# SyncE's transfers kept in source order up to step 16, and one weight load asked for a step later, in a one-core adaLN + S4D + token-mixer kernel

## The chip, the cores and the metric

The kernel runs on one core of a Trainium2 chip, as one launch. The metric is the device time of that core in microseconds (us). Before the change three runs gave 663.74, 665.47 and 670.17 us; the median, 665.47 us, is the time to compare with. Below, PE is the matmul engine, DVE VectorE, ACT ScalarE, POOL GpSimd and SP SyncE, which computes nothing here and issues nearly all transfers between DRAM and on-chip memory.

## The reference

One sequence of L = 2048 tokens with D = 448 channels goes through two blocks, each with a layer norm that is scaled and shifted by vectors made from a condition `c`:

```python
mod = (silu(c) @ w_mod).reshape(1, 6, 1, 448)          # six modulation vectors of 448
sa, ca, ga, sb, cb, gb = (mod[:, k] for k in range(6))
h = layernorm(x) * (1 + ca) + sa
x = x + ga * s4d(h)                                     # long convolution, kernel of N = 256 states
h = layernorm(x) * (1 + cb) + sb
x = x + gb * mixer(h)                                   # gelu(W1 . h + b1), W2: 2048 -> 1792 -> 2048 tokens

def s4d(u):                                             # per channel d
    A, C = -exp(log_A_real) + 1j * A_imag, (C_real + 1j * C_imag) * exp(log_dt)
    K = 2 * real(sum_n C[d, n] * exp(A[d, n] * dt[d] * pos))       # pos = 0 .. 2047
    return causal_convolution(u, K) + u * D_skip
```

## The kernel before, in words

**The steps.** The convolution kernel K is made for 16 channels at a time, in 28 groups `g` of two half groups each, so 56 steps `s`. A step needs two products that PE forms from small tables: exponents (tile `lex`, 4 buffers, group `g` in buffer `g % 4`) and phases (tile `lph`, 3 buffers, group `g` in `g % 3`). ACT turns them into magnitudes and sines, POOL multiplies the tile `G` (L734, L735), DVE the tile `E` (L736 to L740), and PE contracts `E` with `G` into `kg` (L761). Steps come in batches of eight: ahead of each batch stands a window (`window(s)` for s = 8, 16, 24, 32) in which the exponentials of all eight steps are taken at once, because sines and exponentials need different tables on ACT.

**What goes on beside the steps.** From the window of step 8 to that of step 16, PE also transforms the input: `u_rows` multiplies a row of `xt` into PSUM, DVE scales the result into a tile `yt` (L592), and each two of these make one store to DRAM, `yu_d<-yt` (L594, 448 KB). There are 32 such rows, hence 16 stores; in the text below they are **store 1 to store 16**. The tiles `yt` have three buffers (stores 3 to 5 borrow room elsewhere and are called `yE`), so from store 9 on, DVE may write the tile of store k only when store k-3 has landed. From step 16 on, these 16 stores are read back (`u_load`) for the next transform (`u_cols`).

**Loads that fall into this stretch.** `load(g, False)` brings the phases of a group two groups ahead, in two transfers: `load_up` (L650, 32 partitions, 32 KB) and `load_lo` (L654, 64 partitions, 64 KB). `load(g, True)` does the same for exponents, and at steps 4, 12, 20 and so on it is called for four groups in a row, eight transfers. `wm_load(k, ...)` (L338) brings the weights of modulation vector k, 784 KB; those of k = 4, 5 and 3 go into rows 0 to 3, 4 to 7 and 8 to 11 of `xt`, once `u_rows` has used these, and are read by PE in the window of step 16 (L534). `par_load(3)` at step 12 brings the last parameters in eight transfers of 32 KB (L291).

**What sets the order.** On PE, ACT, DVE and POOL the instructions stand in the order of the source for the whole program. SP has that order only inside a context named `first`; outside of it, a scheduler places SP's instructions when the program is built, by when it thinks each can go. The context is entered early in the program and closed by `first.close()` in the loop over steps. The table `late` says at which step a weight load is called:

```python
if s % 2 == 0 and 0 < s and s // 2 + 2 < NG:
    load(s // 2 + 2, False)
if s == 8:
    first.close()
if s in late:
    late[s]()
if s % BATCH == 0:
    (late_window if s > 32 else window)(s)
```

SP works its list in order: an instruction that waits holds all behind it. Besides what its data need, nearly every transfer of SP waits for an earlier one: SP has eight completion semaphores that it uses in turn, and a transfer waits until the one eight places ahead of it in SP's list has landed.

Of the kernel before, what the change touches and what calls it, by code (L numbers as in the profile page):

```python
# [21 lines left out]
L, D, N, F = 2048, 448, 256, 1792  # L22
# [210 lines left out]
def tile_adaln_s4d_mixer(ctx, tc, i, out):  # L233
# [19 lines left out]
    with ExitStack() as es:  # L253
# [44 lines left out]
        PP = 112  # L298
# [6 lines left out]
        xt = xp.tile([P, 16, D], F32, name="xt")  # L305
# [30 lines left out]
        def wm_load(k, tile):  # L336
            wms[k] = tile
            nc.sync.dma_start(wms[k], i["w_mod"][:, k * D : (k + 1) * D].rearrange("(q p) d -> p q d", p=PP))  # L338
# [11 lines left out]
        def wm_slot(k):  # L350
# [16 lines left out]
            ],  # L367
            12: lambda: wm_load(4, xt[0:PP, 0:4, 0:D]),
            13: lambda: wm_load(5, xt[0:PP, 4:8, 0:D]),
            14: lambda: wm_load(3, xt[0:PP, 8:12, 0:D]),  # L370
        }


# [8 lines left out]
        def flush(todo):  # L382
            while todo:
                todo.pop(0)()
# [160 lines left out]
        def u_stats(r):  # L545
            st = xp.tile([P, 6], F32, tag="st", name="st", bufs=2)
            V.bn_stats(st, xt[:, r])
            V.bn_aggr(mv[:, r], st)
# [107 lines left out]
        def load(g, exps):  # L656
            load_up(g, exps)
            load_lo(g, exps)
# [12 lines left out]
        def warm(n):  # L671

            g = made_k[0] // 2
            free = (kgs[g - 1] if g - 1 in kgs else kg_tile(g))[:, 4:8]
            for _ in range(n):
                T.matmul(free, ones[:, 0:P], ones[:, 0:256], start=made_k[0] % 2 == 0, stop=made_k[0] % 2 == 0, skip_group_check=True)
# [7 lines left out]
        def st_exponents(s):  # L684
            g, h = divmod(s, 2)
            phs[s] = [pph.tile([P, 512], F32, tag=nm, name=nm) for nm in ("xe", "xg")]
            halves(phs[s], lex[g % 4][:, h * P : (h + 1) * P], tab[:, 2], True, True)
# [7 lines left out]
        def st_phase(s):  # L695

            g, h = divmod(s, 2)
            lhs = lph[g % 3][:, h * P : (h + 1) * P]
            pm = [pph.tile([P, 512], F32, tag=nm, name=nm) for nm in ("xe", "xg")]
            halves(pm, lhs, tab[:, 1], True, False)  # L700
            halves(pm, mg[:, 0], ones, False, False)
            halves(pm, mg[:, 1], ones, False, False)
            halves(pm, lhs, tab[:, 0], False, True)
            phs[s] = pm
# [43 lines left out]
        def mellow():  # L748
            ready.extend(fresh)
            fresh.clear()  # L750

        def st_kgen(s, to=act):
            g, h = divmod(s, 2)
            kg = kg_tile(g)
            made_k[0] += 1
            E, Gt = eg.pop(s)
            for m in range(4):
                for c in range(2):
                    for q in range(4):
                        d = 8 * (q // 2) + 2 * m + q % 2  # L760
                        T.matmul(  # L761
                            kg[32 * q : 32 * q + 32, m],
                            Gt[:, c, d],
                            E[:, c, d],
                            start=h == 0 and c == 0 and m == 0,
                            stop=h == 1 and c == 1,
                            skip_group_check=True,
                        )
            if h == 1:
                p, o = divmod(g, 2)  # L770
                if o == 0:
                    kss[p] = wp.tile([P, 2, 4, NJ], F32, tag="ks", name="ks")

                def copy():
                    (V.tensor_copy if to is dve else S.copy)(kss[p][:, o], kgs.pop(g)[:, 0:4])
                    if o:
                        dve.append(skip)

                def skip():
                    k0 = kss[p][:, :, :, 0:1]  # L780
                    G.tensor_tensor(k0, k0, dsk[:, g - 1 : g + 1, :, None], ALU.add)
                    fresh.append(p)

                to.append(copy)
# [62 lines left out]
        def pc_load(n):  # L847
            if n < NP:
                pc_u(n)
                pc_w(n)  # L850
            else:
                pc_u(2 * n - NP)
            pc_ahead(n - 4)
# [184 lines left out]
        def more(n):  # L1038

            for _ in range(n):  # L1040
                if next(rest, None) in ("logs", "end"):
                    return
# [120 lines left out]
        for s in range(NHALF):  # L1163
            if s == 32:
                early.close()
                fp = es.enter_context(tc.tile_pool(name="fp", bufs=2))
                m2p.append(right("m2l", BATCH - 3))
                yks[1] = fp.tile([P, 32, DC], F32, name="yk1", bufs=1)
                for n in range(3):
                    pc_load(n)  # L1170
            if s % 2 == 0 and 0 < s and s // 2 + 2 < NG:
                load(s // 2 + 2, False)
            if s == 8:
                first.close()
            if s in late:
                late[s]()
            if s % BATCH == 0:
                (late_window if s > 32 else window)(s)
                if s == 0:
                    gp_ = right("gp", 3)  # L1180
            if s % BATCH == 4:
                for g in range(s // 2 + 2, min(s // 2 + 6, NG)):
                    load(g, True)

            if s == 5:
                late_steps.append(True)

            def between():
                flush(dve)
                if 2 <= s < BATCH:  # L1190
                    for r in range(2 * s, 2 * s + 2):
                        u_stats(r)
                if s < len(pace):
                    more(pace[s])

            mellow()
            if True:
                if s < 32 and s % BATCH > 1:
                    st_kgen(s - 2)
                if s % BATCH == 1 or s < 24 and s % BATCH == 0:  # L1200
                    warm(10)
                if (s + 1) % BATCH:
                    st_phase(s + 1)
                elif s + 1 < NHALF:
                    st_exponents(s + 1)
                if s == 7:
                    warm(10)

                due.extend(soon)
                soon.clear()  # L1210
                if s > 32 and s % BATCH:
                    st_kgen(s - 1, soon)
                if s in (40, 48):
                    piece(True)
                    flush(dve)
                st_step(s, between)
                if s in (40, 48):
                    piece(False, True)
            if s == NHALF - 1:
                break  # L1220
            flush(act)

            if s in (1, 2):
                x_load(4 + 4 * s, 4, G)
            if s in (23, 31):
                idle(10)
            held = s > 32 and s % BATCH == BATCH - 2
            free = s > 7 and not st_s1(hold if held and s + 2 < NHALF else dve if s % BATCH == BATCH - 1 else act)
            if s + 2 < 32 and (s + 2) % BATCH > 1 and s + 2 > 5:
                st_mag2(s + 2)  # L1230

            if 3 < s < 8:
                modulation(s // 2 - 1, s % 2)
            if s == 7:
                par_load(2)

            if 8 <= s < 16 and free:
                some(u_rows, rows, 2 if s % 2 else 3)
            if s == 12:
                par_load(3)  # L1240
            if s == 16:
                spec.close()
                up = early.enter_context(tc.tile_pool(name="up", bufs=2))
                for n in range(4):
                    u_load(n)
                sp3 = early.enter_context(tc.tile_pool(name="sp3", bufs=1))
                s2_load(2, 8, sp3)
            if 17 <= s < 32 and free:
                some(u_cols, cols, 1)
            if s == 31:  # L1250
                flush(dve)
                flush(act)
            if s > 32 and not held and s not in (40, 48):
                piece(s % 2 == 1, back=s % BATCH != BATCH - 1)
            if s == 34:

                for t in (ft, b1, b2):
                    V.memset(t, 0.0)
                nc.sync.dma_start(ft, i["FT"])
                nc.sync.dma_start(b1, i["B_b1"].rearrange("(t p) -> p t", p=P))  # L1260
                nc.sync.dma_start(b2, i["B_b2"].rearrange("(t p) -> p t", p=P))
# [117 lines left out]
    with ExitStack() as es:  # L1379
# [169 lines left out]
        for t in range(16):  # L1549
            ss = slice(t * P, (t + 1) * P)  # L1550
            xt = ru.tile([P, D], F32, tag="x2", name="x2")
# [42 lines left out]
```

## Time and profile before

| what | value |
|---|---|
| median of the runs | 665.47 us (663.74, 665.47, 670.17) |
| the profiled execution's own time | 666.04 us |
| its span, first to last instruction | 664.3 us |
| mean granted TensorE clock | 0.987 |
| moved by DMA | 125.14 MB, mean 188 GB/s |

The span is what the profile's positions count in: "at 104.05" means 104.05 us after the first instruction. The 1.7 us between span and time lie outside of all instructions. A row of the timeline is: start, us (first start to last end of the rows merged in it), engine, line, operation, out<-in, how many, and in brackets the idle time of the engine before it and what ended that. For SP, whose rows are issues only, the start says when SP issued the transfer and not when the data arrived; the arrival is seen from who waited for it.

### The profile page before, as it was taken

The page shows a single profiled execution, that of the slowest core. Times are in us where ns is not written, and L with a number is a line of the kernel's source. Part 1 is how long each engine was busy: PE and PEld are TensorE (multiplying, and loading weights), DVE is VectorE, ACT ScalarE, POOL GpSimd, SP SyncE. Part 2 cuts the span into 40 slices and gives each one's busy share as a digit, 9 for nine tenths or more (in the row PEclk, how much of TensorE's full clock was granted, in tenths as well). Part 3 has the DMA queues.
Part 4 walks back from the last instruction along what each step waited for, and adds up shares of the span by engine and source line. Part 5 has one row for each costly group of instructions (what it writes and reads, how often), then busy time and mean ns, then how long its engine had stood idle before and what let it go on. Part 6 is the DMA issues. An engine that isn't in the chain of part 4 may idle for free.

```text
span 664.3 us, 19155 instructions
## 1 busy us (share of the span) xinstructions
PE 612.2 (92%) x7639; PEld 442.8 (67%) x7639; DVE 444.1 (67%) x852; ACT 440.9 (66%) x828; POOL 269.5 (41%) x350
## 2 busy tenths in 40 slices
PE   1868998999999999999898999999999999999997
PEld 0544455445455555656554667788999999999997
DVE  8999889798893877868665677787522553333331
ACT  6978898999889999999587578886222532222220
POOL 7885597498599788797562000000000000000000
PEclk9999999999999999999999989999999999999999
DMA  6695747598876457676787999946665165555530
GB/s 159 195 222 171 271 136 245 213 269 238 230 263 190 66 160 204 186 210 193 236 279 218 257 241 232 218 117 195 181 179 149 59 197 165 162 160 163 166 113 28
DMA packets 98833, 125.14 MB, mean 188 GB/s; under 512 B 13780, under 2 KB 80120, under 8 KB 98744
## 3 DMA queue, kind: packets, MB, share of 16 engines
q1 hardware_dynamic: 97928, 121.30, 64.6%
q0 software_dynamic: 816, 2.62, 1.6%
q8 instruction: 60, 0.98, 0.7%
q14 instruction: 29, 0.24, 0.1%
HBM read 88.53 MB, written 34.87 MB: 186 GB/s over the span
## 4 chain that ended last, share of the span: by engine, by line
PE 58%; ACT 11%; DMA 10%; DVE 7%; POOL 6%; issue 4%; SPq 2%; DVEq 0%; ACTq 0%; POOLq 0%
PE o L1560 7%; PE o L1562 7%; PE o L1561 7%; PE acc L1397 6%; PE acc L1398 6%; PE acc L1399 6%; PE xe L664 5%; PE kg L761 4%; DMA us_d<-uo 3%; PE xg L664 2%; POOL G L734 2%; DMA w<-in_B_w_dram 2%; POOL G L735 2%; PE vv L892 2%; ACT mag L693 2%
## 5 line engine op out<-in xcount | busy, mean ns | idle before, releaser
L218 ACT CAST whi<-w 128x896 fp32r<-128x896 f32 x64 | 59.7, 939 | 138.6 <-PE o L1561 81.5
L227 DVE TENSOR_TENSOR wlo<-w,whi 128x896 fp32r<-128x896 f32 x64 | 68.1, 1086 | 41.8 <-ACT whi L218 38.7
L734 POOL TENSOR_TENSOR G<-mag,gs 128x512 f32<-128x512 f32 x56 | 71.9, 1284 | 37.4 <-ACT gs L730 37.4
L1397 PE MATMUL acc<-h3h,whi 128*128 128x448 f32 x224 | 83.7, 374 | 3.0 <-ACT h3h L1470 1.4
L1398 PE MATMUL acc<-h3l,whi 128*128 128x448 f32 x224 | 81.9, 365 | 0.4 <-DVE mean L1418 0.2
L1399 PE MATMUL acc<-h3h,wlo 128*128 128x448 f32 x224 | 81.6, 364 | 0.0
L1560 PE MATMUL o<-uh,whi 128*128 128x448 f32 x224 | 81.3, 363 | 0.0
L1562 PE MATMUL o<-uh,wlo 128*128 128x448 f32 x224 | 81.2, 362 | 0.0
L1561 PE MATMUL o<-ul,whi 128*128 128x448 f32 x224 | 80.6, 360 | 0.0
L761 PEld LDWEIGHTS kg<-E,G 128*32 128x32 f32 x3584 | 54.2, 111 | 32.9 <-issue 20.9
L735 POOL TENSOR_TENSOR G<-mag,gs 128x512 f32<-128x512 f32 x56 | 72.0, 1287 | 0.0
L761 PE MATMUL kg<-E,G 128*32 128x64 f32 x3584 | 63.5, 222 | 7.5 <-issue 5.4
L664 PE MATMUL xg<-tab,lph 64*128 64x512 f32 x112 | 62.2, 555 | 7.0 <-DVE E L740 3.0
L1565 DVE TENSOR_TENSOR y<-o,x 128x448 f32<-128x448 f32 x16 | 10.0, 625 | 78.8 <-PE o L1562 78.8
L664 PE MATMUL xe<-tab,lph 64*128 64x512 f32 x112 | 62.2, 555 | 0.4 <-issue 0.4
L714 POOL TENSOR_TENSOR m<-mag,w 128x512 f32<-128x512 f32 x53 | 55.8, 1052 | 4.2
L1397 PEld LDWEIGHTS acc<-h3h,whi 128*128 128x128 f32 x224 | 42.5, 190 | 16.2 <-ACT h L1469 3.5
L1398 PEld LDWEIGHTS acc<-h3l,whi 128*128 128x128 f32 x224 | 42.4, 189 | 3.4 <-DVE h3l L1467 0.5
L1399 PEld LDWEIGHTS acc<-h3h,wlo 128*128 128x128 f32 x224 | 42.4, 189 | 3.3
L1562 PEld LDWEIGHTS o<-uh,wlo 128*128 128x128 f32 x224 | 42.1, 188 | 3.4
L1561 PEld LDWEIGHTS o<-ul,whi 128*128 128x128 f32 x224 | 41.9, 187 | 3.0
L1560 PEld LDWEIGHTS o<-uh,whi 128*128 128x128 f32 x224 | 42.0, 188 | 2.1
(256 smaller groups left out, 1391.5 us busy)
## 6 DMA issues: line engine op xcount, KB each, us to landing
w<-in_B_w_dram SPq DMA_DIRECT2D x64, 224.0 KB
w<-in_B_w_dram SPq DMA_DIRECT2D x32, 448.0 KB
yi<-yu_d SPq DMA_DIRECT2D x32, 224.0 KB
us_d<-uo SPq DMA_DIRECT2D x16, 448.0 KB
u<-us_d SPq DMA_DIRECT2D x64, 112.0 KB
v_d<-vt SPq DMA_DIRECT2D x32, 224.0 KB
vt<-v_d SPq DMA_DIRECT2D x14, 448.0 KB
yu_d<-yt SPq DMA_DIRECT2D x13, 448.0 KB
```

Source lines behind the costliest of these rows:

```text
L218: self.nc.scalar.copy(hi, w)
L227: eng.tensor_tensor(lo, w, hi.bitcast(F32), ALU.subtract)
L664: T.matmul(out[k], lhs[r], rhs[r], start=start, stop=stop)
L734: G.tensor_tensor(Gt[:, 1], mg_, v32(sg), ALU.mult)
L735: G.tensor_tensor(Gt[:, 0], mg_, v32(cg_), ALU.mult)
L761: T.matmul(kg[32 * q : 32 * q + 32, m], Gt[:, c, d], E[:, c, d], start=h == 0 and c == 0 and m == 0, stop=h == 1 and c == 1, skip_group_ch ...
L1397: nc.tensor.matmul(acc[f], hi[:, fs], h3h[:, r], start=r == 0, stop=False)
L1398: nc.tensor.matmul(acc[f], hi[:, fs], h3l[:, r], start=False, stop=False)
L1399: nc.tensor.matmul(acc[f], lo[:, fs], h3h[:, r], start=False, stop=r == 15)
L1560: nc.tensor.matmul(o, hi[:, ks], uh[kh][:, k], start=kh == 0 and k == 0, stop=False)
L1561: nc.tensor.matmul(o, hi[:, ks], ul[kh][:, k], start=False, stop=False)
L1562: nc.tensor.matmul(o, lo[:, ks], uh[kh][:, k], start=False, stop=kh == 1 and k == 6)
```

## The change

The closing of the context `first` moves from step 8 to step 16, so SP's transfers that are called between the two keep the order of the source instead of the scheduler's. The weights of modulation vector 3 are called at step 15 instead of step 14. Nothing is added or taken away, and the four other engines have the same instructions in the same order.

```diff
@@ -367,7 +367,7 @@
             12: lambda: wm_load(4, xt[0:PP, 0:4, 0:D]),
             13: lambda: wm_load(5, xt[0:PP, 4:8, 0:D]),
-            14: lambda: wm_load(3, xt[0:PP, 8:12, 0:D]),
+            15: lambda: wm_load(3, xt[0:PP, 8:12, 0:D]),
         }
@@ -1170,7 +1170,7 @@
             if s % 2 == 0 and 0 < s and s // 2 + 2 < NG:
                 load(s // 2 + 2, False)
-            if s == 8:
+            if s == 16:
                 first.close()
             if s in late:
                 late[s]()
```

SP's list before, from store 7 to store 11; the first wait of a row is for the transfer eight places ahead (`DMAHW` 0 to 7 are the eight semaphores), a wait for DVE or PE is for data. `lph_141` holds the phases of group 8, `xt<-in_w_mod_dram` is here the load for vector 5.

```order
L594 DMA yu_d<-yt 128x896 [waits DMAHW1_49,DVE_49]
L650 DMA lph_141<-pars_58 32x256 [waits DMAHW2_49,PE_49]
L654 DMA lph_141<-pars_58 64x1x256 [waits DMAHW3_49,PE_49]
L338 DMA xt<-in_w_mod_dram 112x4x448 [waits DMAHW4_49,PE_49]
L594 DMA yu_d<-yt 128x896 [waits DMAHW5_49,DVE_49]
L594 DMA yu_d<-yt 128x896 [waits DMAHW6_49,DVE_49]
L650 DMA lph_139<-pars_58 32x256 [waits DMAHW7_49,PE_49]
L654 DMA lph_139<-pars_58 64x1x256 [waits DMAHW0_49,PE_49]
L594 DMA yu_d<-yt 128x896 [waits DMAHW1_49,DVE_49]
L594 DMA yu_d<-yt 128x896 [waits DMAHW2_49,DVE_49]
```

Stores 8 and 9 stand together behind one weight load; the weight load for vector 4, the eight exponent loads of groups 8 to 11 and the eight parameter loads all stand further ahead, between stores 3 and 7. Now, SP's list from the phases of group 8 (just behind store 8) to store 9:

```order
L650 DMA lph_141<-pars_58 32x256 [waits DMAHW2_49,PE_49]
L654 DMA lph_141<-pars_58 64x1x256 [waits DMAHW3_49,PE_49]
L338 DMA xt<-in_w_mod_dram 112x4x448 [waits DMASW6_49,DMASW5_49,DMAHW4_49,DMASW4_49,DMASW3_49]
L650 DMA lex_142<-pars_58 32x256 [waits DMAHW5_49]
L654 DMA lex_142<-pars_58 64x1x256 [waits DMAHW6_49]
L650 DMA lex_143<-pars_58 32x256 [waits DMAHW7_49]
L654 DMA lex_143<-pars_58 64x1x256 [waits DMAHW0_49]
L650 DMA lex_144<-pars_58 32x256 [waits DMAHW1_49]
L654 DMA lex_144<-pars_58 64x1x256 [waits DMAHW2_49]
L650 DMA lex_145<-pars_58 32x256 [waits DMAHW3_49]
L654 DMA lex_145<-pars_58 64x1x256 [waits DMAHW4_49]
L594 DMA yu_d<-yt 128x896 [waits DMAHW5_49,DVE_49]
```

Step 12's calls now stand as a block between store 8 and store 9: the weights of vector 4, then the exponents of four groups. The last exponent load shares its semaphore, `DMAHW4`, with the weight load. Behind store 9 come the eight parameter loads of step 12, and then, from the last of them on:

```order
L291 DMA A_A_imag<-in_A_A_imag_dram 64x128 [waits DMAHW5_49]
L338 DMA xt<-in_w_mod_dram 112x4x448 [waits DMAHW6_49,PE_49]
L594 DMA yu_d<-yt 128x896 [waits DMAHW7_49,DVE_49]
L594 DMA yu_d<-yt 128x896 [waits DMAHW0_49,DVE_49]
L650 DMA lph_139<-pars_58 32x256 [waits DMAHW1_49,PE_49]
L654 DMA lph_139<-pars_58 64x1x256 [waits DMAHW2_49,PE_49]
L594 DMA yu_d<-yt 128x896 [waits DMAHW3_49,DVE_49]
L338 DMA xt<-in_w_mod_dram 112x4x448 [waits DMASW7_49,DMAHW4_49,DMASW0_49,PE_49]
L594 DMA yu_d<-yt 128x896 [waits DMAHW5_49,DVE_49]
```

The last parameter load waits on the semaphore of store 9 (`DMAHW5`); then come the weights of vector 5, stores 10 and 11, the phases of group 9, store 12, the weights of vector 3 and store 13. DVE's rows of steps 14 and 15, the same as before but for the numbers of the semaphores:

```order
L592 SCALAR_TENSOR_TENSOR yt<-pu,means,mod_105 128x448 [waits DMAHW5_49,PE_49]
L592 SCALAR_TENSOR_TENSOR yt<-pu,means,mod_105 128x448 [waits PE_49]
L739 TENSOR_TENSOR E<-mag,xg 128x16x32 [waits Activation_49]
L740 TENSOR_TENSOR E<-m_1638,xg 128x16x32
L736 TENSOR_TENSOR E<-m_1729,xe 128x16x32 [waits PE_49,Activation_49,Pool_49]
L737 SCALAR_TENSOR_TENSOR E<-mag,xe 128x16x32
L592 SCALAR_TENSOR_TENSOR yt<-pu,means,mod_105 128x448 [waits DMAHW7_49,DVE_49,PE_49]
```

The first row writes the tile of store 12 and waits for store 9 (`DMAHW5`); the last writes that of store 13 and waits for store 10 (`DMAHW7`).

## The prediction

> **What bounds the kernel now.** I read the page first, then the busy times of the stretches that the stores touch, then the chain of waits there, then the timelines of DVE and SP. From the page:
>
> ```profile
> span 664.3 us, 19155 instructions
> GB/s 159 195 222 171 271 136 245 213 269 238 230 263 190 66 160 204 186 210 193 236 279 218 257 241 232 218 117 195 181 179 149 59 197 165 162 160 163 166 113 28
> PE 58%; ACT 11%; DMA 10%; DVE 7%; POOL 6%; issue 4%; SPq 2%; DVEq 0%; ACTq 0%; POOLq 0%
> ```
>
> Transfers are 10% of the chain over the whole span, so an order of transfers can matter somewhere. The stretches (us, then busy time and count of PE, PEld, DVE, ACT, POOL, then clock, DMA share, GB/s):
>
> ```profile
> 82.00:114.00 32.00, 30.01 (x616) 17.51 (x614) 28.55 (x48) 27.92 (x56) 29.29 (x32) 1.00 0.63 202
> 114.00:130.00 16.00, 15.28 (x254) 7.22 (x254) 11.66 (x25) 14.56 (x31) 8.53 (x15) 1.00 0.56 205
> ```
>
> Steps 8 to 15 are 82 to 114: PE, POOL and DVE are all busy for about nine tenths, so none can absorb a stall of several us. In the window of step 16 (114 to 130) PE idles 0.7 us and ACT 1.4. The chain of waits through the end of the first stretch:
>
> ```profile
> 107.31 1.28 POOL G L734
> 108.58 1.23 POOL G L735
> 109.82 0.18 POOL ks L781
> 110.01 0.68 DVE E L736
> 110.69 0.60 DVE E L737
> 111.29 1.78 DVE yt L592 x3
> 113.07 0.59 DVE E L739
> 113.66 0.61 DVE E L740
> 114.41 0.47 PE xg L664
> 114.87 1.03 PE kg L761 x64
> 115.91 0.95 PE pu L588 x4
> ```
>
> Up to 110 POOL's products set the pace. From 110.01 it is DVE: the first E products of step 15, then three rows of `yt` at 111.29, then the rest of step 15, then PE. So DVE's time at 111 is on the path that sets the end. No transfer is on this piece; the change cannot gain by taking one off it. It can only put one on.
>
> DVE's rows that write `yt`:
>
> ```profile
> 94.15 1.86 DVE L592 SCALAR_TENSOR_TENSOR yt<-pu,means,mod 128x448 f32<-128x448 f32 x3
> 104.05 1.28 DVE L592 SCALAR_TENSOR_TENSOR yt<-pu,means,mod 128x448 f32<-128x448 f32 x2 [1.49 <-DMA yu_d<-yt]
> 107.63 1.27 DVE L592 SCALAR_TENSOR_TENSOR yt<-pu,means,mod 128x448 f32<-128x448 f32 x2
> 111.21 1.86 DVE L592 SCALAR_TENSOR_TENSOR yt<-pu,means,mod 128x448 f32<-128x448 f32 x3
> ```
>
> The pair at 94.15 fills store 8, the pair at 104.05 store 11, at 107.63 store 12, and the first two at 111.21 store 13. Three buffers make DVE wait three stores back. It did once, 1.49 us at 104.05, for store 8, whose issue is in SP's rows:
>
> ```profile
> 94.49 0.38 SPq L650 DMA_DIRECT2D lph<-pars  x1
> 94.96 0.56 SPq L654 DMA_DIRECT2D lph<-pars  x1
> 95.61 0.40 SPq L338 DMA_DIRECT2D xt<-in_w_mod_dram  x1
> 96.11 3.25 SPq L594 DMA_DIRECT2D yu_d<-yt  x2
> 105.84 0.34 SPq L338 DMA_DIRECT2D xt<-in_w_mod_dram  x1
> ```
>
> Store 8 went out at 96.11, right behind 784 KB of weights at 95.61, and landed at about 104.05: 8.4 us from the load's issue to the store's landing. This is what a store costs that stands behind a weight load, and the change rearranges just that.
>
> **The change part by part.** *Store 8 moves ahead of the weight loads.* It is issued when its second row is done, 94.15 + two rows of 0.62 = 95.4, with nothing large in front. The 1.49 us wait at 104.05 goes. What is late next is POOL, which set the pace there up to 110, so this gains between 0 and 1.5 us if nothing else waits. I take 0, because of what follows.
>
> *Store 9 moves behind step 12's block.* Behind store 8 SP issues two phase loads and then the weights of vector 4. By the spacing of the rows above (94.49 to 95.61) that load goes at 95.4 + 0.5 + 1.1 = 97.0. It landed, in the analogous place, before the store behind it: 8.4 us less that store's own share. 448 KB at the 279 GB/s of the page's busiest slice are 1.6 us, so 6.8 us; it lands at 103.8. The eighth transfer behind it, the last lower half of the exponents, needs the same semaphore and cannot go sooner. The same order (weights, then four groups of exponents) stands in the trace at step 4:
>
> ```profile
> 41.83 0.33 SPq L338 DMA_DIRECT2D wm<-in_w_mod_dram  x1
> 42.99 0.31 SPq L650 DMA_DIRECT2D lex<-pars  x1
> 43.35 0.48 SPq L654 DMA_DIRECT2D lex<-pars  x1
> ...
> 53.22 0.51 SPq L654 DMA_DIRECT2D lex<-pars  x1
> ...
> 57.86 0.40 SPq L338 DMA_DIRECT2D wm<-in_w_mod_dram  x1
> 58.30 0.55 SPq L360 DMA_DIRECT2D svt<-in_SV_dram  x1
> 59.41 0.80 SPq L606 DMA_DIRECT2D s<-in_S_dram  x2
> ```
>
> The row at 53.22 is the eighth behind that at 41.83, and the first row at 59.41 the eighth behind 53.22. That SP stood still for it shows in its waits:
>
> ```profile
> SPq L654 <- DMA wm<-in_w_mod_dram: 3.9, 2, 2.3
> ```
>
> So the weights had landed at 53.22, and the fourth lower half at about 59.41, 6.2 us later, or 1.55 us for each of the four lower halves (64 KB each), far below the rate of a wide transfer. [...]
>
> [...] The duration in the trace is used.
>
> Store 9 is issued just behind the fourth lower half and lands at 103.8 + 6.2 + its own share: 110.0 with no share of its own, 111.6 with all 1.6 us. I take 111.0. In the trace of before, DVE wrote the tile of store 12 at 107.63; it must now wait until 111.0. First stall: 3.4 us (2.4 to 4.0). All of DVE's list is behind it, the E products of steps 14 and 15 first.
>
> *Store 10 moves behind vector 5's weights.* Its second row is at 101.9 in the trace of before, so its data are ready long before. But SP is held: the last of the eight parameter loads waits for store 9's landing, 111.0. The next row, the weights of vector 5, goes at 111.6 and store 10 right behind. From a weight load's issue to the landing of the store behind it I have 8.4 us, with one lower half queued in front of it; here none is, so 8.4 - 1.55 = 6.9. Store 10 lands at 111.6 + 6.9 = 118.5. DVE wrote the tile of store 13 at 111.21: it is now 7.3 us late, first stall included. Bounds: 110.6 + 6.9 = 117.5, so 6.3 late; 112.2 + 8.4 = 120.6, so 9.4 late. I take 7.3, nearest to the rows above.
>
> *What the lateness costs.* It sits at 111.29 of the chain above, with half of step 15's E products behind it on DVE, then PE's `xg`, which needs them at 114.41. ACT keeps working meanwhile on the exponentials' beginning, and the window's idle time (0.7 us of PE, 1.4 of ACT) can take up a little: I take 1.0 (0.5 to 1.5). What follows starts from this window's results, the read-back included:
>
> ```profile
> 128.95 0.33 SPq L407 DMA_DIRECT2D pars<-hl  x1
> 130.53 5.18 SPq L614 DMA_DIRECT2D yi<-yu_d  x8
> ```
>
> The `yi` loads stand in SP's list behind the last parameter store of the window, which DVE's list feeds, and shift with it. So the delay runs through to the end: 7.3 - 1.0 = 6.3 us.
>
> *The rest costs nothing.* The weights of vector 4 are issued at 97.0 instead of early in the window of step 8, those of vector 5 at 111.6 instead of 95.61, those of vector 3 later than 105.84. PE uses them, and the phases of group 8, here:
>
> ```profile
> 118.28 0.94 PE L534 MATMUL pm<-xt,scb 112*32 112x448 f32 x8
> 122.46 0.96 PE L534 MATMUL pm<-xt,scb 112*32 112x448 f32 x8
> 127.03 0.96 PE L534 MATMUL pm<-xt,scb 112*32 112x448 f32 x8
> ```
>
> Vector 4 arrives at 103.8 for 118.28; vector 5 at 118.5 - 1.6 = 116.9 for 122.46 + 6.3. Vector 3 is asked for behind store 12, at about 113.6; in front of it in the queues are stores 11 and 12 (1.6 each) and a lower half (1.55) behind store 10's 118.5, so 123.3, and its own 784 KB at 279 GB/s are 2.9: 126.2 for 127.03 + 6.3 = 133.3. The move from step 14 to 15 lets store 12 go first; left at 14 it would have to be issued ahead of it. That is worth something against its absence, but not against before.
>
> **The rivals.** *R1, no queueing: a small gain.* If transfers behind the lower halves are spread such that they pass them, store 9 lands in time, the 1.49 us go, and the gain is between 0 and 1.5: about 664.7. [...] Chance 0.12.
>
> *R2, only one stall.* The first stall comes, but vector 5's weights find the queues empty and store 10 lands within 3 us of its issue at 112.0: then DVE is 3.8 us late at most, and with 1.0 absorbed the time is 2.4 to 2.8 us more, about 668.3. For it: 784 KB in 3 us would be no more than the 279 GB/s; against it: the 8.4 us above. Chance 0.20.
>
> *R3, slower: the weights of vector 3 come too late.* PE's list holds the product at 127.03 ahead of step 16's phases, so a late load would stop PE, and all behind it. It decides from the point where the load lands after 133.3, 7.1 us later than worked out. If the queues cost as much again as in the step-4 rows (another 6.2 for lower halves, 8.4 instead of 6.9 for the pair with store 10, as much for store 12), it lands at about 136, and the time is 3 us over the forecast's: 674.8. Chance 0.08.
>
> **How the numbers follow.** Against the profiled execution, 666.04 + 6.3 = 672.3; that execution lies 0.57 over the median of the runs, so 671.8 against 665.47, or +0.95%. This is the likeliest case, chance 0.60; its own range is 669.5 to 674 (lateness 6.3 to 9.4, absorbed 0.5 to 1.5, with the upper end as rare as its row). About 1% is what a measurement of this kernel can tell from no change, 6.7 us here, so the forecast sits on the edge: of its 0.60 I count 0.32 as slower and 0.28 as same. With R3 (0.08) slower is 0.40. Same is 0.28 + R2's 0.20 + 0.07 of R1 = 0.55. Faster by over 1% has no mechanism; R1's remainder, 0.05, stands for what I have not seen. The range, 665.5 to 675.5, leaves out most of R1 and half of R3.
>
> **What would show it.** In the changed kernel's profile: no wait at the pair of store 11; DVE waiting on `yu_d<-yt` about 3.4 us for store 12's tile and again, about 4, for store 13's; vector 4's weights issued near 97 and vector 5's near 111.6; the chain of waits with `yu_d<-yt` on it between 105 and 119; everything from 130 on shifted by one amount, about 6. Wrong would be: no wait of DVE there (R1), a single one (R2), PE waiting for `xt` at the third modulation product (R3), or a window of step 16 that is shorter by several us and gives the delay back.

## The result, and the profile after

The changed kernel takes 676.25 us (median of 675.58, 676.24, 676.25 and 677.58) against 664.61 us for the kernel before in the same series: 1.016 times, with a 95% interval of 1.012 to 1.020. The forecast was 671.8 and its range ended at 675.5. The kernel before, timed again beside the experiments, had medians of 667.06, 667.04 and 665.86 us with single runs from 662.0 to 672.6, so the first comparison met it near its lower side; against 667 the loss is 9 us.

The page of the profiled execution after, which took 677.58 us:

```profile
span 675.8 us, 19152 instructions
PE 66%; DMA 11%; ACT 9%; DVE 7%; issue 4%; SPq 1%; POOL 1%; ACTq 0%; DVEq 0%; POOLq 0%
```

The shares of the whole chain hide the change: DMA goes from 10% to 11%. The rows of DVE that write `yt` show it:

```profile
104.24 1.87 DVE L592 SCALAR_TENSOR_TENSOR yt<-pu,means,mod 128x448 f32<-128x448 f32 x3
114.37 1.28 DVE L592 SCALAR_TENSOR_TENSOR yt<-pu,means,mod 128x448 f32<-128x448 f32 x2 [5.87 <-DMA yu_d<-yt]
121.69 1.87 DVE L592 SCALAR_TENSOR_TENSOR yt<-pu,means,mod 128x448 f32<-128x448 f32 x3 [3.66 <-DMA yu_d<-yt]
```

The wait for store 8 is gone from the tile of store 11 (104.24). In its place are 5.87 us for store 9 and 3.66 us for store 10, at the tiles that the prediction named. The chain of waits after, from the weights of vector 4 on:

```profile
99.39 7.53 DMA xt<-in_w_mod_dram
106.92 0.02 issue
106.94 0.50 SPq L654
...
107.54 6.73 DMA yu_d<-yt
...
114.37 0.19 DVE yt L592
114.56 0.41 issue
114.97 0.52 DVE yt L592
115.48 6.08 DMA yu_d<-yt
...
121.69 1.29 DVE yt L592 x2
122.98 0.04 issue
123.02 1.98 PE y L799 x62
...
125.73 1.86 PE kg L761 x64
```

This is the mechanism of the two stalls in one column: the weights land at 106.92, which lets the last lower half go; store 9 follows at 107.54 and takes 6.73 us; store 10 takes 6.08 us. The chain's step from 114.37 to 115.48 is not quite right: store 10's data were written long before. SP's own rows show what held it:

```profile
107.54 0.37 SPq L594 DMA_DIRECT2D yu_d<-yt  x1
...
113.17 1.59 SPq L291 DMA_DIRECT2D A_A_imag<-in_A_A_imag_dram  x2
114.85 0.53 SPq L338 DMA_DIRECT2D xt<-in_w_mod_dram  x1
115.48 0.91 SPq L594 DMA_DIRECT2D yu_d<-yt  x2
```

The second parameter load of the row at 113.17 waits until store 9 lands (114.27, the end of the chain's 6.73 us); the weights of vector 5 go at 114.85, and store 10 behind them.

The last row of the chain shows something that the prediction does not have: `kg` takes 1.86 us where it took 1.03 before. The busy times of the stretches, after (columns as above):

```profile
105.00:120.00 15.00, 9.37 (x150) 5.35 (x148) 7.16 (x12) 6.87 (x14) 9.68 (x11) 0.71 0.48 138
120.00:130.00 10.00, 7.57 (x205) 5.69 (x207) 6.72 (x11) 7.17 (x13) 2.37 (x4) 0.59 0.89 318
```

PE is busy for 9.37 of 15 us, and its granted clock is 0.71 and then 0.59 where it was 1.00 in both stretches before.

**A measure that the scatter blurs less.** The same instruction of POOL, the first product `G` of step 10 and that of step 16, before and then after:

```profile
90.93 1.28 POOL L734 TENSOR_TENSOR G<-mag,gs 128x512 f32<-128x512 f32 x1
133.06 1.27 POOL L734 TENSOR_TENSOR G<-mag,gs 128x512 f32<-128x512 f32 x1 [4.13 <-ACT gs L730]
```

```profile
93.29 1.28 POOL L734 TENSOR_TENSOR G<-mag,gs 128x512 f32<-128x512 f32 x1
144.76 1.28 POOL L734 TENSOR_TENSOR G<-mag,gs 128x512 f32<-128x512 f32 x1 [4.14 <-ACT gs L730]
```

From step 10 to step 16 it is 42.13 us before and 51.47 after: 9.34 more. The 2.36 us by which step 10 itself is later are left out: the experiments below show shifts of that size there in the kernel before as well, from one execution to the next. In this document "the stretch" is this distance; what it gains over 42.13 is nearly what the expectations call "the shift that arises between step 8 and step 17", which they put at 9.0 us for the changed kernel. One profile used below, that of the kernel before with wide lower halves, is of an execution that was slow for its kernel (671.79 us against a median of 667.52).

### The profile page after: what moved, and what is told of

It is laid out like the page before. It is cut to its first block, busy times and chain, and to the rows that moved or that the text cites. A ratio compares the mean times of both kernels' runs of the same rounds, so it can differ in the third digit from the quotient of the medians.

```text
span 675.8 us, 19152 instructions
## 1 busy us (share of the span) xinstructions
PE 617.0 (91%) x7639; PEld 445.5 (66%) x7639; DVE 443.2 (66%) x852; ACT 441.1 (65%) x828; POOL 268.5 (40%) x350
## 4 chain that ended last, share of the span: by engine, by line
PE 66%; DMA 11%; ACT 9%; DVE 7%; issue 4%; SPq 1%; POOL 1%; ACTq 0%; DVEq 0%; POOLq 0%
PE xe L664 7%; PE o L1560 7%; PE o L1562 7%; PE o L1561 7%; PE kg L761 6%; PE acc L1397 6%; PE acc L1398 6%; PE acc L1399 6%; DMA w<-in_B_w_dram 3%; PE xg L664 3%; PE pu L624 2%; PE pu L588 2%; DMA yu_d<-yt 2%; DMA v_d<-vt 2%; PE vv L892 2%
## 5 line engine op out<-in xcount | busy, mean ns | idle before, releaser
L761 PEld LDWEIGHTS kg<-E,G 128*32 128x32 f32 x3584 | 57.2, 115 | 35.5 <-issue 22.1
L761 PE MATMUL kg<-E,G 128*32 128x64 f32 x3584 | 67.1, 228 | 8.1 <-issue 5.6
L736 DVE TENSOR_TENSOR E<-m,xe 128x512 f32<-128x512 f32 x53 | 36.2, 683 | 12.8 <-ACT xe L729 5.6
L726 ACT ACTIVATE ab<-xe 128x512 f32<-128x512 f32 x56 | 33.9, 605 | 15.8 <-PE xg L664 9.7
```

The source lines that it names most:

```text
L761: T.matmul(kg[32 * q : 32 * q + 32, m], Gt[:, c, d], E[:, c, d], start=h == 0 and c == 0 and m == 0, stop=h == 1 and c == 1, skip_group_ch ...
```

## The experiments

All profiled executions, cut at the same two instructions (start to step 10, stretch, rest to the end of the span), with DVE's waits at the tiles of stores 11, 12 and 13, which are the waits for stores 8, 9 and 10:

| kernel | median us | ratio to before, 95% | start / **stretch** / rest, us | DVE waits for stores 8 / 9 / 10, us |
|---|---|---|---|---|
| before | 665.47 | | 90.93 / **42.13** / 531.24 | 1.49 / 0 / 0 |
| before, again | 670.01 (one run) | | 92.98 / **45.03** / 530.19 | 1.71 / 0 / 0 |
| vector 3 at step 15 only | 666.6 | 0.995–1.003 | 91.26 / **44.88** / 528.76 | 1.67 / 0 / 0 |
| before, wide lower halves | 667.52 | 0.996–1.003 | 96.11 / **43.01** / 530.88 | 1.29 / 0 / 0 |
| after | 676.25 | 1.012–1.020 | 93.29 / **51.47** / 531.04 | 0 / 5.87 / 3.66 |
| after, again | 676.86 | 1.008–1.022 | 95.27 / **50.81** / 530.72 | 0 / 5.16 / 4.52 |
| order kept to 16 only | 675.8 | 1.007–1.020 | 90.68 / **51.20** / 527.62 | 0 / 5.38 / 4.11 |
| after, early exponents | 669.13 | 0.998–1.005 | 91.88 / **45.04** / 530.68 | 0 / 0 / 2.42 |
| after, wide lower halves | 675.4 | 1.004–1.016 | 94.59 / **52.08** / 530.33 | 0 / 4.06 / 6.41 |
| after, stalls filled | 676.7 | 1.007–1.019 | 97.72 / **53.25** / 527.93 | 0 / 5.52 / 4.10 |
| after, filled longer | 673.79 | 1.007–1.019 | 89.38 / **50.96** / 527.76 | 0 / 5.21 / 4.55 |
| after, vector 5 at step 15 | 676.17 | 1.011–1.021 | 92.17 / **49.10** / 534.13 | 0 / 5.54 / 0 |
| after, both moved | 668.51 | 1.002–1.008 | 91.20 / **45.38** / 529.32 | 0 / 0 / 0 |

The start varies by 8 us and the rest by 6 in kernels that do the same work there; the stretch is 42.1 to 45.0 in the four with the old order and 50.8 to 51.5 in the three with the new order and nothing else.

**Both kernels again.** The changed kernel and the kernel before, unchanged:

> The changed kernel once more, for what of its first profile repeats. Theory A (two waits of DVE for stores 9 and 10, and a TensorE clock halved because of them): the two waits again (5.9 and 3.7 us, within 1 us each), a clock drop that begins while PE stands still between 105 and 115, time 674 to 678. Theory B (part of the 11.6 us is chance): the shift of 2.4 us that was there before step 8 began, with a clock drop at 66.8, does not come again, and the time is near 673. A drop at 66 to 70 that comes again would say that the change reaches further ahead than SP's list shows.

> The kernel before once more, for a second profile: how far the places of its steps move from run to run. The part up to step 8 moves by up to 4 us, as in the changed kernel's two profiles (2.4 and 4.3 us); from step 8 to 17 it is within 3 us of the first profile, with one wait of DVE (1.5 us, store 8).

After: the two waits come again (5.16 and 4.52 us), and the stretch is 50.81. Before: no wait but that for store 8, and a stretch of 45.03, 2.9 us longer than in its first profile. So the first profile of before, from which the whole prediction was worked out, showed this stretch at its shortest.

**Which half of the change.** Once the closing of `first` alone, once the weights of vector 3 alone. Against the kernel before:

```diff
-            if s == 8:
+            if s == 16:
                 first.close()
```

> Source order up to step 16, but the weights of vector 3 at step 14 again, so ahead of store 12. Theory A: stores 9 and 10 are where the changed kernel has them, so the two waits and 10 to 13 us over before, the same as the changed kernel; store 12 lands some 3 us later, which is worth at most 2 us more. A rival by which the step of vector 3's weights matters (PE waiting for xt at its product): 3 us or more over the changed kernel.

```diff
-            14: lambda: wm_load(3, xt[0:PP, 8:12, 0:D]),
+            15: lambda: wm_load(3, xt[0:PP, 8:12, 0:D]),
```

> The scheduler's order from step 8 on, only the weights of vector 3 at step 15. Theory A: within 0.3% of before, 663 to 667, no wait of DVE for stores 9 and 10. The rival that the later weights cost something by themselves: PE waits at the third modulation product of step 16's window, 2 us or more over before.

The first alone gives the whole loss (675.8 us, stretch 51.20; 8.7 us over the kernel before in its series, a little under the expected 10 to 13), the second nothing (666.6 us, 44.88).

**The exponents out of store 9's way.** The changed kernel, with the exponents of groups 8 to 11 asked for at step 9 and not at step 12, so that no lower half stands between the weights of vector 4 and store 9:

```diff
-            if s % BATCH == 4:
-                for g in range(s // 2 + 2, min(s // 2 + 6, NG)):
+            if s % BATCH == 4 and s != 12 or s == 9:
+                for g in range(8, 12) if s == 9 else range(s // 2 + 2, min(s // 2 + 6, NG)):
```

> The changed kernel, but the exponents of groups 8 to 11 are loaded at step 9 instead of step 12, so the four lower halves stand ahead of store 7 and no more between the weights of vector 4 and store 9. Theory A: store 9 lands about 1.6 us after the weights of vector 4, near 106, DVE does not wait for it or less than 1 us; SP is not held at the last parameter load, the weights of vector 5 go near 106 and store 10 lands near 113: a second wait of 0 to 2 us. Time 664 to 668. The rival by which it is the weights alone that delay store 9: the first wait stays over 3 us and the time over 672.

SP's rows of this kernel and DVE's remaining wait:

```profile
98.00 0.34 SPq L338 DMA_DIRECT2D xt<-in_w_mod_dram  x1
99.97 0.34 SPq L594 DMA_DIRECT2D yu_d<-yt  x1
...
106.55 0.53 SPq L338 DMA_DIRECT2D xt<-in_w_mod_dram  x1
107.18 1.41 SPq L594 DMA_DIRECT2D yu_d<-yt  x2
```

```profile
107.01 1.27 DVE L592 SCALAR_TENSOR_TENSOR yt<-pu,means,mod 128x448 f32<-128x448 f32 x2
113.08 1.28 DVE L592 SCALAR_TENSOR_TENSOR yt<-pu,means,mod 128x448 f32<-128x448 f32 x2 [2.42 <-DMA yu_d<-yt]
```

Store 9 now goes out at 99.97, still behind the weights of vector 4, and nobody waits for it. With that the parameter loads and the weights of vector 5 come 6.9 us sooner (106.55 against 114.85, less the 1.4 by which this execution's step 10 is earlier), and the wait for store 10 shrinks to 2.42 us. The stretch is 45.04, the time 669.13 us, a little over the expected 664 to 668: 6 of the 7 to 9 us come back by moving eight small transfers. Store 10 still pays for standing behind 784 KB: 5.9 us from its issue at 107.18 to the end of the wait at 113.08.

**Is it the narrow form of the lower halves?** Each `load_lo` as two transfers of 32 partitions, in the changed kernel and in the kernel before:

```diff
-            nc.sync.dma_start(t[64:128], src[1:3])
+            nc.sync.dma_start(t[64:96], src[1])
+            nc.sync.dma_start(t[96:128], src[2])
```

> The changed kernel, each lower half loaded as two transfers of 32 partitions, the form of the upper halves, instead of one of 64. If the narrow transfers are what holds store 9 (theory A): the twelve exponent transfers land within about 0.3 us of each other behind the weights of vector 4, store 9 lands 2 to 4 us after these weights instead of 7.4, the first wait falls from 5.4 to 0 to 3 us, and the shift from step 8 to 17 from 9.0 to 2 to 6. Rival (the number of transfers or the weights hold it): the first wait stays over 4 us.

> The kernel before, with the same two transfers for each lower half. The lower halves cost something elsewhere too, by its chain of waits (lph<-pars 4.5 us and lex<-pars 7.1 us near 234 to 245): theory A expects them gone from the chain and the time 2 to 6 us below before. Rival (what is late next behind them comes at the same time, or SP's longer list costs as much): within 1 us of before.

In the changed kernel the loss stays (675.4 us, stretch 52.08), though the first wait is shorter. SP's rows and DVE's:

```profile
101.25 0.33 SPq L338 DMA_DIRECT2D xt<-in_w_mod_dram  x1
...
108.77 1.80 SPq L654 DMA_DIRECT2D lex<-pars  x1
110.61 0.42 SPq L655 DMA_DIRECT2D lex<-pars  x1
111.13 0.37 SPq L594 DMA_DIRECT2D yu_d<-yt  x1
...
116.66 0.53 SPq L338 DMA_DIRECT2D xt<-in_w_mod_dram  x1
117.29 0.91 SPq L594 DMA_DIRECT2D yu_d<-yt  x2
```

```profile
113.85 1.28 DVE L592 SCALAR_TENSOR_TENSOR yt<-pu,means,mod 128x448 f32<-128x448 f32 x2 [4.06 <-DMA yu_d<-yt]
123.93 1.87 DVE L592 SCALAR_TENSOR_TENSOR yt<-pu,means,mod 128x448 f32<-128x448 f32 x3 [6.41 <-DMA yu_d<-yt]
```

Store 9 takes only 2.7 us now, from 111.13 to the end of the wait at 113.85, against 6.73 us, with no narrow transfer ahead. But it is issued 9.9 us behind the weights and not 8.15, because SP has twelve transfers to issue in between, at 0.3 to 0.5 us each, and still waits for the one eight places ahead. What the transfers no longer take, SP's list takes. Theory A's first wait of 0 to 3 us is missed, and the rival's sign, over 4 us, is just met. In the changed kernel the DMA share is 0.26 over the last part of store 9's way behind the narrow transfers (110.50 to 114.27), and 0.92 from the issue of store 10 behind the weights of vector 5 to its landing (115.48 to 121.57). Which of the DMA engines a transfer uses is not shown. In the kernel before the wide form gains nothing (667.52 us); its wait for store 8 is 1.29 us.

**The weights of vector 5 out of store 10's way.** The changed kernel, with

```diff
-            13: lambda: wm_load(5, xt[0:PP, 4:8, 0:D]),
-            15: lambda: wm_load(3, xt[0:PP, 8:12, 0:D]),
+            15: lambda: [wm_load(5, xt[0:PP, 4:8, 0:D]), wm_load(3, xt[0:PP, 8:12, 0:D])],
```

> Only the place of one transfer differs from the changed kernel: the weights of the fifth vector are asked for at step 15 instead of step 13, so that stores 10, 11 and 12 stand ahead of them in SyncE's queue. Theory A (the second wait is store 10 queued behind these weights, which themselves wait for store 9): the first wait at the yt rows, for store 9's tile, stays at 5 to 6 us, the second falls from 3.7-4.5 us to under 1 us, the shift that arises between step 8 and step 17 falls from 9.0 us to 4.4-6 us, and the time is 671 to 673. Rival B (the second wait comes from the first: store 10's data are themselves made late, because VectorE was stopped at step 14): the second wait stays at 3 us or more, and the time at 675 to 677.

```profile
112.90 1.28 DVE L591 SCALAR_TENSOR_TENSOR yt<-pu,means,mod 128x448 f32<-128x448 f32 x2 [5.54 <-DMA yu_d<-yt]
116.48 1.86 DVE L591 SCALAR_TENSOR_TENSOR yt<-pu,means,mod 128x448 f32<-128x448 f32 x3
122.91 1.27 DVE L591 SCALAR_TENSOR_TENSOR yt<-pu,means,mod 128x448 f32<-128x448 f32 x2 [0.23 <-PE pu L587]
128.26 1.28 DVE L591 SCALAR_TENSOR_TENSOR yt<-pu,means,mod 128x448 f32<-128x448 f32 x2 [3.77 <-PE pu L587]
```

The second wait is gone, so it was store 10 behind these weights, as theory A has it and rival B does not. But the gain is not there: DVE waits 3.77 us for PE in the window instead, the stretch is 49.10 (A: 46.5 to 48.1), and the time 676.17 us. The chain of waits of this kernel says what became late:

```profile
116.09 1.91 PE kg L760 x64
118.00 0.02 issue
118.03 0.37 ACT ks L774
...
119.04 1.28 ACT L497
...
121.07 1.28 ACT L503
...
123.41 0.50 PE xe L663
```

Behind the first wait, ACT's own list from `kg` to the first magnitudes takes 5.4 us (118.03 to 123.41, two loads of function tables of 1.28 us each among it), and PE's exponents need these. With one stall of 5 us this list is the next thing that is late; it had been hidden behind the second stall. A part of its lateness is PE's clock: from DVE's row to the end of `kg` it is 5.06 us here (112.90 to 117.96), where `kg` takes 1.94 us and the mean granted clock from 105 to 120 is 0.66, and 3.38 in the kernel "after, filled longer" below (110.26 to 113.64), where `kg` takes 1.10 us and the clock is 1.00. By an estimate from these two executions the lower clock took 1.7 us of the missing gain; without them the stretch would be about 47.4, inside A's range. No run with this order at full clock shows it. That the rest of the program is also 3 us longer than in the changed kernel (534.13) is one execution, and was not followed up.

**Both moved.** The exponents at step 9 with the edit shown above, and the weights of vector 5 at step 14, behind stores 10 and 11:

```diff
-            13: lambda: wm_load(5, xt[0:PP, 4:8, 0:D]),
+            14: lambda: wm_load(5, xt[0:PP, 4:8, 0:D]),
```

> The changed kernel with the exponents of groups 8 to 11 asked for at step 9, ahead of the weights of the fourth vector, and the weights of the fifth vector asked for at step 14, behind stores 10 and 11. Theory A (the loss consists of what stands ahead of stores 9 and 10 in SyncE's queue): no wait over 0.5 us at the yt rows for the tiles of stores 9 and 10, the shift that arises between step 8 and step 17 under 3 us, and a time of 664 to 669, the same as before within 0.5%. Rival (the order of the source costs elsewhere too, on the loads of step 17 that then come later): stores 9 and 10 wait for nothing, but a load of step 17 or 18 ends a wait of 2 us or more, and the time is 670 to 674.

Stores 9 and 10 stop nobody, and the time is 668.51 us, 1.005 times before: inside the expected 664 to 669, though a little slower than before (interval 1.002 to 1.008), and the stretch is 45.38 (3.25 over the first profile, where under 3 was expected). What is left is neither theory's:

```profile
118.14 0.68 DVE L592 SCALAR_TENSOR_TENSOR yt<-pu,means,mod 128x448 f32<-128x448 f32 x1 [1.20 <-DMA yu_d<-yt]
123.74 1.28 DVE L592 SCALAR_TENSOR_TENSOR yt<-pu,means,mod 128x448 f32<-128x448 f32 x2 [4.65 <-PE pu L588]
```

The wait has moved on to store 12, which now stands behind the weights of vector 5: 1.20 us, and then DVE waits 4.65 us for PE. PE itself stands still for 2.22 us in the middle of a `kg` there (from 117.18), for which the profile names no cause; this was not followed up. No order tried here beat the kernel before.

**What the halved clock costs.** Filler matmuls on PE, whose results nobody reads, at steps 14 and 15: first 48 and 20, then 48 and 42 (the second number in the diff):

```diff
+            if s in (14, 15):
+                warm(48 if s == 14 else 42)
```

> The changed kernel with 48 and 20 matmuls of ones (0.125 us each, 6.0 and 2.5 us) put at steps 14 and 15 just where PE stands still for DVE's two waits; they write a part of a PSUM tile that nothing reads. Theory A (the waits cost 8.1 us of DVE's time, and the halved clock that they bring adds 0.3 to 1.2 us in the window of step 16 where 1.0 would have been absorbed): the two waits as before, the granted clock stays at 1.0 from 105 to 130, PE's rows in the window of step 16 at full speed (kg near 1.03 us for 64 and not 1.9), and the shift from step 8 to step 17 falls from 9.0 to 7 to 8 us; time 672 to 676. Rival (the clock costs nothing, since PE waits for DVE anyway): shift of 8.5 us or more. Rival (the clock costs most of it): shift under 5 us.

> The changed kernel with filler matmuls whose results nobody reads, 48 at step 14 and 42 at step 15, at 0.113 us each about 5.4 and 4.7 us, the length of VectorE's two waits, so that TensorE isn't idle in either. Theory A (after the waits the halved clock of TensorE costs what my sum missed): granted clock 1.00 from 105 to 136, waits of VectorE as before within 0.5 us, and the shift that arises between step 8 and step 17 at 7 to 8.5 us instead of 9.0; time 674 to 676. Rival (the clock costs nothing there, since VectorE sets the pace of the window): the shift stays at 9 us with the clock at 1.00. Should the filler itself end later than the waits, the shift grows instead, and the run says nothing on the clock.

With 20 at step 15 the filler ends 2.4 us before the wait does, the clock is halved from 129.2 to 136.1 us (0.51 and 0.50 in the two pieces up to 136.0), and the stretch is 53.25. With 42 it is not:

```profile
105.00:136.00 31.00, 29.67 (x482) 18.87 (x478) 17.54 (x35) 19.78 (x38) 13.95 (x21) 1.00 0.69 234
```

```profile
110.26 1.28 DVE L592 SCALAR_TENSOR_TENSOR yt<-pu,means,mod 128x448 f32<-128x448 f32 x2 [5.21 <-DMA yu_d<-yt]
118.47 2.04 DVE L592 SCALAR_TENSOR_TENSOR yt<-pu,means,mod 128x448 f32<-128x448 f32 x3 [4.55 <-DMA yu_d<-yt]
```

The clock is 1.00 throughout, and yet the stretch is 50.96: by its total the rival is right, and the clock is not the main part of the loss. By place it has a part. From DVE's three rows at the tile of store 13 (118.47 here, 121.69 after, 111.21 before) to `G` of step 16 (140.34, 144.76, 133.06) it is 21.87 us with the fillers, 23.07 after and 21.85 before. So at full clock the window takes as long as before. With pieces at half rate in it, it is 1.2 us longer in the first profile of after, 0.4 in the second and 0.3 in the kernel with the order alone (granted clock 0.59, 0.57 and 0.83 from 120 to 130), and 2.9 longer in the run with 20 fillers, where the half rate lasts from 129.2 to 136.1 (126.20 to 150.97 is 24.77). Against that, store 10 came 0.7 us later here than after (28.40 us from `G` of step 10 to the row at 121.69 after, 89.38 to 118.47 = 29.09 here), which may be in part why the total does not show it. The kernel before, again has 22.52 us in this window at a clock of 1.00, so one execution of each cannot settle differences under 0.7 us.

## Why the prediction was right or wrong

**The mechanism was right.** Both waits came at the tiles named, with the weights of vector 4 and the lower halves ahead of store 9, and store 9's landing ahead of the weights of vector 5 and of store 10. Moving the exponents away took the first wait, moving vector 5's weights the second. R1 (no queueing) and R2 (one stall) are out: store 9 needed 6.73 us, and store 10 landed 6.7 us after the weights ahead of it were issued (114.85 to 121.57). R3 is out as well: PE nowhere waits for the weights of vector 3.

**The first stall: 4.4 us for 3.4 (2.4 to 4.0).** DVE's row is at 114.37 against 107.63, less the 2.36 us of the start. The weights were issued where forecast (99.39 - 2.36 = 97.03 for 97.0) but took 7.53 us for 6.8; from their landing to store 9's it was 7.35 us (106.92 to 114.27) for 7.2. So the term of the weights was 0.7 us too small: it had been worked out by taking a store's share at the rate of the page's busiest slice off a measured 8.4. The sum lets the lower halves go one after the other and store 9 end behind the last of them; which engines they use, and whether that is why the store ends late, no run shows. What the runs showed is the time: with each lower half in two transfers of 32 partitions the store took 2.7 us and not 6.73. The 1.55 us for each from step 4, with 1.0 us for the store itself, gave the 7.2 and so was a good price.

**The second: 8.1 us for 7.3 (6.3 to 9.4).** From G of step 10 to DVE's row it is 28.40 us after and 20.28 before (28.54 and 29.01 in the other two). The step from store 9's landing to the weights (0.58 us for 0.6) and from there to store 10 (6.72 for 6.9) held; the 0.8 us over are the first stall's.

**The step that failed is what the window takes up.** I let it absorb 1.0 us (0.5 to 1.5) out of idle time of PE and ACT. Against the profile from which the sum was worked out it absorbed nothing: from DVE's row to step 16's `G` it is 21.87 us at full clock against 21.85 before. A likely reason, argued and not tested: idle time of ACT ahead of PE's next result is no slack when what comes late is the very input that both wait for. And in the three executions of the new order it is 0.3 to 1.2 us longer, with pieces at half rate in it, which no term of the sum had. 8.1 + 1.2 = 9.3 us instead of 6.3; against the 666.04 us of the profiled execution that is 675.4, and less its 0.57 over the median, 674.8, inside the range. The means say the same of the absorption and less of the clock. From `G` of step 10 to DVE's row it is 21.43 us in the mean of the four executions of the old order and 28.65 in the three of the new, from there to step 16's `G` 22.34 and 22.51. So the lateness is 7.2 us, near the 7.3, and of the 1.0 us nothing is absorbed. One of the four old-order windows shows half rate as well (vector 3 at step 15 only, where `kg` takes 1.90 us at 116.62), and the windows of the new order are only 0.2 us longer in the mean.

**The rest of the distance is open.** The profile of before shows the stretch at 42.13 us; in three more executions with the old order it was 43.0 to 45.0. Against the mean of the four, 43.8, the three of the new order (mean 51.2) lose 7.4 us, not far over the 6.3. The medians lose 9 to 12, with an interval of 8 to 13 in the first series and 5 to 15 in the second; which part of the 2 to 4 us between them and the stretch is scatter of the start and the rest, these runs don't settle. That the 7.2 us of the means lies so near the 7.3 is partly luck: the sum started from the shortest of the four old executions, and its first stall was 1.0 us too small against that one.

**Costs counted at nothing.** Store 8's wait went and gained nothing, as counted. The weights of vectors 4, 5 and 3 were in time. That vector 3 at step 15 "is worth something" against its absence isn't to be seen: 675.8 us without, 676.25 and 676.86 with.

**The chances.** Slower by over 1% came true at 0.40, where "same" had 0.55. Putting the forecast on the edge was sound; spreading its terms evenly about it wasn't, since the two things not thought of, no absorption and a lower clock, both make it slower.

## What to carry to other kernels

A store on which a ring of buffers turns should not stand in a queue behind a large load, and still less behind that and many small ones: here the 784 KB of vector 4 alone stopped nobody at store 9, and moving the eight small loads behind them three steps ahead gave back 6 us. Price what follows a stall as late by the whole stall, unless the row that absorbs it doesn't need what is late; idle time in a stretch is no such row by itself, as here, where the window took 21.87 us at full clock behind the stalls and 21.85 without them. Before blaming a change for a shift, cut two executions of the same kernel at the same instructions: the one stretch that differs more between kernels than between executions is where to look.

## What the runs showed of the hardware

**The clock falls after less than a full stall.** In the profiles of before and after, the changes of the granted clock lie whole multiples of 3.41 us apart; after, it falls to 0.50 at 111.22 and is back at 1.00 at 128.28, 17.06 us later. The busy time of PE in pieces of that length, with clock, DMA share and GB/s, after and then before, again:

```profile
107.81:111.22 3.41, 1.66 (x10) 1.00 0.50 179
111.22:114.63 3.41, 0.00 (x0) 0.50 0.26 79
```

```profile
104.00:107.41 3.41, 2.03 (x11) 1.00 0.76 295
107.41:110.80 3.39, 3.39 (x68) 0.50 0.69 207
```

In the second kernel PE had been busy for 2.03 of 3.41 us, stopped by 1.38 us of waiting for DVE after store 8, and the next 3.4 us ran at half rate (0.50): here a piece that was three fifths busy came ahead of a fall of the clock. No border in busy time comes out of these runs: a piece with 2.36 us busy (113.30 to 116.70, vector 3 at step 15 only) was followed by half rate (`kg` 1.90 us at 116.62, 1.10 at 111.50), one with 2.25 us (122.40 to 125.80, after, stalls filled) by full rate (1.00 from 125.80 to 129.20). The old order's stretch goes with it in three executions: the two with pieces at half rate in it have 45.03 and 44.88 us, the first profile of before, at 1.00 throughout, 42.13, all three with a wait of 1.5 to 1.7 us for store 8.

**SP's own time counts.** An issue that waits for nothing takes SP 0.3 to 0.6 us in the rows shown, so the twelve exponent transfers of the wide form occupy it for 9.9 us (101.25 to 111.13) with the waits for the transfer eight places ahead. Splitting narrow transfers into more wide ones made store 9's own passage 4 us shorter and its issue later by nearly half of that.
